# A fused attention and gated-MLP kernel: the output weights loaded earlier, one batch's loads moved back, and more PSUM copies on ScalarE

## The chip, the cores and the metric

The kernel runs on one core of a Trainium2 chip. The metric is the device time of one execution in microseconds (us). TensorE multiplies matrices (PE in the profile, its weight loads PEld), VectorE is DVE, ScalarE is ACT, GpSimd is POOL, and SyncE (SP) only issues DMAs here. Each engine runs its own instructions in program order and waits on semaphores for the others.

## The reference

Eight batches, 12 heads, 448 tokens, head dimension 64. First attention with normalised queries and keys, then a gated MLP in which half of the hidden channels are mixed over the tokens:

```python
q_n, k_n = (rmsnorm(q, g_q), rmsnorm(k, g_k))
scores = scale * np.matmul(q_n, k_n.transpose(0, 1, 3, 2))
attn = softmax(scores)
x = (attn @ v).transpose(0, 2, 1, 3).reshape(B, S, H * D)
h = np.maximum(x @ w_in, 0.0)
u, v = (h[..., :d_ff // 2], h[..., d_ff // 2:])
v_n = (v - mu) / np.sqrt(var + 1e-06)
v_s = np.einsum('ts,bsd->btd', w_spatial, v_n) + b_spatial[None, :, None]
out = (u * v_s) @ w_out
```

(The softmax is written short.) Inputs and output are float32; the matrix products run on bf16.

## The kernel before, in words

**Groups and steps.** The 12 heads of a batch are worked in three groups of four, so there are 24 groups G, three for each batch. A group has seven score pieces of 128 rows. From piece 20 on, pieces are taken in pairs, and one pair is a *step* s, from 10 to 83: a group is 3.5 steps, a batch 10.5. Every step writes its scores into one four-bank PSUM tile, `pss` (L365 and L361), and one exponential on ACT (`expo`, L372) turns it into `et`. As there is only one `pss`, the scores of a step wait for the exponential of the step before. When a group's pieces are through, `attend` (L411) makes the row sums and the weighted values on PE (L394), the reciprocal on ACT (L400, L401) and the product `xt` on DVE (L408). These are the *busy* steps (11, 14, 18, 21 and so on).

**Preparation of q and k.** Each group's q and k go through squares (L237 on POOL, a few on ACT at L235), a reduction on DVE (L245), the inverse root on ACT (L253, L254) and a scaling to bf16, `n`, on POOL (L264). They are then transposed. For the first groups PE does it (L271, copied out on DVE at L278 and L285). From group 6 on SP issues a DMA transpose (L339): q lands straight in `qT`, k lands in `kr`, and DVE scales it into `kT` (L345). A table `todo` says in which step each of these happens, in the order `ks, red, rstd, sc, sq, turn, tr, ld` within a step. For the groups from 9 on, with m = G // 2, an even group's transposes stand in steps 7m-5 and 7m-4, an odd one's in 7m-3 and 7m-2. Groups 6 and 7 have their own: both of group 6 in step 18, both of group 7 in step 20; group 8 has steps 23 and 24, group 9 has 25 and 26.

**Loads of q and k.** Each `load_part` (L107) is one DMA issued from SP. Batch 3 is cut into 22 parts: ten in steps 16 and 17, twelve in steps 21 to 24, three a step. From batch 4 on a batch is ten larger parts, three a step: batch 4 in steps 24 to 27, batch 5 in 34 to 37, batch 6 in 45 to 48. Batches share two buffers in turn, so batch 4 goes where batch 2 was. Within a step, transposes stand before loads, and the stores of finished outputs (`flush`, L529 and L531) come after them, all on SP's one queue.

**The MLP as filler.** Between a step's scores and those of the next, PE is given matmuls of the MLP from a list, `work`, in the steps that aren't busy. `gated(b)` puts a batch's units there: v units (L473), u units (L503), for batch 0 the four PE transposes of the spatial weights (`w_sp_unit`, L205 to L213), for later batches the output units of the batch before (L545), and then the spatial units (L513). Batch 0 is put on the list in step 12, batch 1 in step 22. All units take their PSUM buffers from one pool of four, `ps`, which `attend` and the PE transposes use too. A unit's result is copied out by `relu` (L442 on ACT, L444 on DVE) or `copy` (L448, L450), and `pick` chooses the engine: ACT while a quota lasts, then DVE. Spatial results are multiplied by u on DVE (L517).

**The rest of the first gated part.** In step 12 the spatial weights are loaded by POOL. In step 16 ACT copies the bias row. In step 19 POOL issues the load of `w_out` (L203), one DMA that also casts to bf16. It is first used by the output units of batch 0 that are mixed into `tails(1)` in step 24. The normalised v (`vn`, L495) is made on POOL.

In the profile, the exponentials show the steps: step 10 begins its exponential at 37.71 us, step 16 at 56.75, 17 at 61.40, 18 at 64.30, 19 at 66.90, 20 at 69.79, 21 at 74.82, 24 at 84.83, 30 at 102.45.

Of the kernel before, what the change touches and what calls it, by code (L numbers as in the profile page):

```python
# [19 lines left out]
def kernel(  # L20
# [21 lines left out]
    B, H, S, D = q.shape  # L42
# [8 lines left out]
    pe, act, dve, pool, sync = nc.tensor, nc.scalar, nc.vector, nc.gpsimd, nc.sync  # L51
# [59 lines left out]
    def load_v(b, parts):  # L111
        t = vts[b % 2].rearrange("p h c d -> p h (c d)")
        for i in parts:
            hs = slice(6, 12) if i > 1 else slice(0, 6)
            r, c, n, x = pieces(v[b][hs])[i]
            pool.dma_start(out=t[r, hs, D * c:D * (c + n)], in_=x)  # L116
# [45 lines left out]
    w_spT = const.tile([P, NT, S], BF)  # L162
# [14 lines left out]
    def dummies(n, ps=ps_d):  # L177
        for _ in range(n):
            pe.matmul(out=ps[:, 0:128], lhsT=ident, rhs=ident, start=True, stop=True)
# [17 lines left out]
    def load_w_sp():  # L197
        pool.dma_start(out=w_sp[:, 0:3], in_=moe_w_spatial[0:SM].rearrange("(p c) s -> p c s", c=3))
        pool.dma_start(out=w_sp[0:64, 3], in_=moe_w_spatial[SM:S])
        sync.dma_start(out=bst[64:65, :], in_=moe_b_spatial.partition_broadcast(1))  # L200

    def load_w_out():
        pool.dma_start(out=w_out, in_=moe_w_out.rearrange("(c p) m -> p c m", p=P))  # L203

    def w_sp_unit(sc):  # L205
        ps = ps_w.tile([P, 8, 128], BF, name="ps")
        n = P if sc < 3 else 64
        cols = slice(sc, SM, 3) if sc < 3 else slice(SM, S)
        for t in range(NT):
            kp = P if t < 3 else 64  # L210
            pe.matmul(out=ps[0:n, t, 0:kp], lhsT=w_sp[0:kp, t, cols], rhs=ident[0:kp, 0:kp],
                      is_transpose=True, start=True, stop=True, tile_position=(0, 0))
        dve.tensor_copy(out=w_spT[0:n, sc, :], in_=ps[0:n].rearrange("p t c -> p (t c)")[:, 0:S])  # L213

    def bias_row():
        row, b = w_spT[64:65, NT - 1, :], bst[64:65, :]
        for o, i in ((row[:, 0:SM].rearrange("o (m r) -> o m r", r=P),
                      b[:, 0:SM].rearrange("o (r m) -> o m r", m=3)), (row[:, SM:S], b[:, SM:S])):
            act.activation(out=o, in_=i, func=AF.Copy, bias=0.0, scale=1.0)
# [132 lines left out]
    def scores(ps, p):  # L352
        G, i = divmod(p, NCH)
        y = int(i > 3)
        for yy in ((0, 1) if i == 3 else (y,)):
            qT, kT = qkt[G, 0, yy], qkt[G, 1, yy]
            for h in range(2):
                r = slice(64 * h, 64 * h + 64)
                if i == 3:
                    c0 = 384 + 64 * yy  # L360
                    pe.matmul(out=ps[64 * yy:64 * yy + 64, h, 0:S], lhsT=qkt[G, 1, 0][r, c0:c0 + 64],  # L361
                              rhs=qT[r, :], start=True, stop=True, tile_position=(64 * h, 64 * yy))
                else:
                    c0 = 128 * (i - 4 * y)
                    pe.matmul(out=ps[:, h, 0:S], lhsT=kT[r, c0:c0 + 128], rhs=qT[r, :],  # L365
                              start=True, stop=True, tile_position=(64 * h, 0))

    def expo(ps, p, m):
        s, a = divmod(p, 2)
        if a == 0:  # L370
            ets[s] = e_pool.tile([P, 4, S], BF, name="et")
        act.activation(out=ets[s][:, 2 * a:2 * a + 2 * m, :], in_=ps[:, 0:2 * m, 0:S],  # L372
                       func=AF.Exp, bias=0.0, scale=1.0)
# [37 lines left out]
    def attend(G):  # L411
        for part in (-1, 0, 1):
            weigh(G, part)
            if part < 0:
                recip(G)
        for half in (0, 1):
            xt_store(G, half)
# [14 lines left out]
    quota = [0]  # L432

    def pick():
        if quota[0] > 0:
            quota[0] -= 1
            return act
        return dve
# [7 lines left out]
    def copy(out, in_):  # L446
        if pick() is act:
            act.activation(out=out, in_=in_, func=AF.Copy, bias=0.0, scale=1.0)  # L448
        else:
            dve.tensor_copy(out=out, in_=in_)  # L450
# [82 lines left out]
    def flush():  # L533
        while stores:
            stores.popleft()()
# [37 lines left out]
    def gated(b):  # L573
        work.extend(unit_v(b, 0) + unit_v(b, 1))
        also(lambda: stats(b, 0))
        work.extend(unit_v(b, 2))
        also(lambda: stats(b, 1))
        work.extend(tails(b))
        also(lambda: stats(b, 2))
        also(lambda: stats(b, 3))  # L580
        work.extend(unit_u(b, 0) + unit_u(b, 1))
        also(lambda: ln_rstd(b))
        for c in range(NT):
            also(lambda c=c: ln_apply(b, c))
        work.extend(unit_u(b, 2) + unit_u(b, 3))
        if b == 0:
            work.extend((0.5, lambda sc=sc: w_sp_unit(sc), True) for sc in range(NT))
        else:
            for c in range(3):
                work.extend(unit_o(b - 1, c, 0) + unit_o(b - 1, c, 1))  # L590
        for f in range(4):
            work.extend(unit_s(b, f))
# [3 lines left out]
    def fill(us_of_pe, whole):  # L596

        debt[0] = min(debt[0] + us_of_pe, us_of_pe)
        while work and (debt[0] > 0 or work[0][0] == 0 or (whole and not work[0][2])):
            cost, fn, _ = work.popleft()  # L600
            debt[0] -= cost
            fn()
# [140 lines left out]
    for b in range(2, B):  # L743
        for n, x in enumerate(BY_GROUP if b < 4 else [divmod(n, 5) for n in range(10)]):
            if b == 2:
                step = S0 + n // 4
            elif b == 3:
                step = 16 + n // 5 if n < 10 else 21 + (n - 10) // 3
            else:
                step = (21 * b - 36) // 2 + n // 3  # L750
            todo.setdefault(step, []).append(("ld", NG * b, x))

    ORDER = ("ks", "red", "rstd", "sc", "sq", "turn", "tr", "ld")
# [1 line left out]
    def prep(s, early_act):  # L755
        for what, G, i in sorted(todo.get(s, ()), key=lambda x: (ORDER.index(x[0]), x[1:2] if x[0] == "ld" else x[1:])):
            if (what == "rstd" and G < 5) != early_act:
                continue
            if what == "ld":
                load_part(G // NG, *i)  # L760
            elif what == "turn":
                transpose_pe(G, i, dve)
            elif what == "sq":
                squares(G, i, eng=act if (G, i) in ((6, 1), (7, 1), (8, 1)) else None)
            elif what == "red":
                reduce(G, i)
            elif what == "rstd":
                rstd(G)
            elif what == "sc":
                scaled(G, i, eng=dve if (G, i) in ((4, 0), (4, 1)) else None)  # L770
            elif what == "tr":
                transpose_dma(G, i)
            elif what == "ks":
                k_scale(G)

    def attend_step(G):
        return (NCH * G + NCH - 1) // 2 + 1
# [6 lines left out]
    busy = {attend_step(G) for G in range(NGT)}  # L784
# [6 lines left out]
    for s in range(S0, NST):  # L791
        scores(pss[:, 0:2], 2 * s)
        scores(pss[:, 2:4], 2 * s + 1)
        prep(s, True)
        expo(pss, 2 * s, 2)
        prep(s, False)
        flush()
        if s == S0:
            dummies(24, ps_w.tile([P, 512], FP, name="ps"))
        if s in v_step:  # L800
            load_v(*v_step[s])
        if s == 12:
            load_w_sp()
        if s == 16:
            bias_row()
        if s == 19:
            load_w_out()
        if s in gate_step:
            b = gate_step[s]
            gated(b)  # L810
            nxt = min(x for x in list(gate_step) + [NST] if x > s)
            n = sum(1 for x in range(s, nxt - 1) if x not in busy)
            rate = sum(w[0] for w in work) / (n + 0.5)
        if s in busy:
            attend([G for G in range(NGT) if attend_step(G) == s][0])
            quota[0] = 0
        else:
            quota[0] = 0 if s + 1 in busy else 1
            fill(rate, s + 1 in busy)


# [7 lines left out]
    n = 0  # L829
# [35 lines left out]
```

## Time and profile before

| | |
|---|---|
| median of 5 runs | 295.58 us (293.1 to 299.78) |
| the profiled execution | 298.54 us, span 296.6 us, mean granted TensorE clock 0.988 |
| PE busy | 271.4 us, 92% of the span |
| DVE busy | 212.0 us, 71% |
| ACT busy | 206.1 us, 69% |
| POOL busy | 199.3 us, 67% |
| the 74 exponentials of the steps (L372) | 123.0 us, 1663 ns each |
| SP's queue and ACT's | 40.32 MB in 74562 packets |
| POOL's queue | 8.66 MB in 21744 packets |

The busy shares are averages. To see what one stage is limited by, look at the waits of the engine that is nearly always busy, and follow what released each of them. In the timeline a line is one or more like instructions: start, time, engine, source line, operation, output and inputs, and in brackets how long the engine had been idle and what ended it. SPq lines are DMAs being issued; the time given there is that of the issue, not of the transfer. The DMA rows of the page give the time from issue to landing:

```profile
qb<-in_q_dram SPq DMA_DIRECT2D x38, 96.0 KB, 5.2
kb<-in_k_dram SPq DMA_DIRECT2D x34, 96.0 KB, 5.9
...
w_out<-in_moe_w_out_dram POOLq DMA_DIRECT2D x1, 768.0 KB, 10.0
...
kr<-n SPq DMA_TRANSPOSE x18, 5.4
```

### The profile page before, as it was taken

Reading aid. Unit: us, or ns where it says so; the run is one execution under the profiler, and the core shown is the slowest. Engines: PE = TensorE matmul, PEld = TensorE weight load, DVE = VectorE, ACT = ScalarE, POOL = GpSimd, SP = SyncE. Lnnn points to the kernel's source line nnn. Section 1 sums busy time; section 2 is a strip of 40 time slices with the busy share of each in tenths; the row PEclk is TensorE's granted clock in tenths of the full one; section 3 lists DMA queues with packets and bytes.
Section 4 is the critical chain, followed back from the end, with each engine's and each line's share of the span. In section 5 each row is a group of like instructions: output and inputs, shape, how many; then the busy total and the mean of one; then the engine's idle time right before and its main releaser. Section 6 shows DMA issues by size and latency. Waiting matters only on the chain.

```text
span 296.6 us, 6614 instructions
## 1 busy us (share of the span) xinstructions
PE 271.4 (92%) x2593; PEld 129.8 (44%) x2601; DVE 212.0 (71%) x369; ACT 206.1 (69%) x262; POOL 199.3 (67%) x192
## 2 busy tenths in 40 slices
PE   8588999688979979999999699999999999999994
PEld 8354554333434434444444333444344444444552
DVE  3978777778479486978897648868897949544553
ACT  2798985886857847876877656967787786673411
POOL 3786768999549959589889849489889850400400
PEclk9999999997999999999999989999999999999999
DMA  7998999986999999998889999999971892030145
GB/s 165 226 225 198 193 216 239 221 149 101 147 219 193 250 226 229 245 194 120 198 145 220 222 183 221 231 153 167 165 96 42 133 226 48 24 137 0 30 159 187
DMA packets 97698, 49.99 MB, mean 169 GB/s; under 512 B 67586, under 2 KB 93955, under 8 KB 97667
## 3 DMA queue, kind: packets, MB, share of 16 engines
q1 hardware_dynamic: 74562, 40.32, 65.9%
q0 software_dynamic: 21744, 8.66, 25.2%
q10 hardware_dynamic: 1360, 0.59, 0.8%
q8 instruction: 20, 0.33, 0.5%
q14 instruction: 12, 0.09, 0.1%
HBM read 38.55 MB, written 11.01 MB: 167 GB/s over the span
## 4 chain that ended last, share of the span: by engine, by line
PE 58%; DMA 17%; DVE 7%; ACT 5%; SPq 5%; issue 3%; POOL 3%; ACTq 0%; POOLq 0%; DVEq 0%
PE ps L394 11%; PE ps L473 11%; PE ps L545 10%; PE ps L503 8%; PE ps L513 7%; PE pss L365 7%; DMA qb<-in_q_dram 6%; DMA kb<-in_k_dram 6%; DMA kr<-n 5%; SPq L107 4%; ACT et L372 3%; DVE ms L245 2%; DVE kT L345 1%; DVE xt L408 1%; PE pss L361 1%
## 5 line engine op out<-in xcount | busy, mean ns | idle before, releaser
L372 ACT ACTIVATE et<-pss 128x1792 bf16<-128x1792 f32 x74 | 123.0, 1663 | 55.0 <-PE pss L365 52.3
L545 PE MATMUL ps<-w_out,gt 128*128 128x384 bf16 (+1 forms) x256 | 47.9, 332 | 5.2 <-DVE osb L450 4.8
L264 POOL TENSOR_TENSOR n<-qb,rs 128x896 bf16<-128x896 f32 x19 | 32.0, 1686 | 29.3 <-ACT rs L254 25.4
L245 DVE TENSOR_REDUCE ms<-sqt 128x14 f32<-128x896 f32 x44 | 47.0, 1076 | 5.3 <-POOL sqt L237 4.8
L408 DVE TENSOR_TENSOR xt<-ps,rc 128x448 bf16<-128x448 f32 x48 | 27.8, 618 | 30.3 <-ACT rc L401 30.2
L473 PE MATMUL ps<-w_in_v,xt 128*128 128x512 bf16 (+1 forms) x184 | 45.1, 381 | 0.4
L503 PE MATMUL ps<-xt,w_in_u 128*128 128x448 bf16 x192 | 40.1, 353 | 3.9 <-DMA w_in_u<-in_moe_w_in_dram 2.1
L394 PE MATMUL ps<-et,vt 128*32 128x448 bf16 x768 | 41.0, 353 | 0.5 <-DVE osb L450 0.5
L365 PE MATMUL pss<-qT,kT 64*128 64x448 bf16 x254 | 37.6, 358 | 2.7 <-DVE kT L345 1.7
L237 POOL TENSOR_TENSOR sqt<-qb 128x896 f32<-128x896 f32 x22 | 37.1, 1685 | 0.2
L545 PEld LDWEIGHTS <-gt 128*128 128x128 bf16 (+1 forms) x256 | 24.2, 101 | 25.9 <-issue 13.3
L450 DVE COPY osb<-ps 128x384 f32<-128x384 f32 (+1 forms) x46 | 25.1, 555 | 11.5 <-PE ps L545 10.5
L264 POOL TENSOR_TENSOR n<-kb,rs 128x896 bf16<-128x896 f32 x19 | 32.2, 1693 | 0.1
L237 POOL TENSOR_TENSOR sqt<-kb 128x896 f32<-128x896 f32 x19 | 31.9, 1680 | 0.0
L513 PE MATMUL ps<-w_spT,vn 128*128 128x448 bf16 (+1 forms) x128 | 29.1, 371 | 1.1 <-DVE w_spT L213 1.0
L116 POOL DMA_DIRECT2D vt<-in_v_dram x40 | 29.1, 731 | 1.2 <-PE pss L365 0.7
L495 POOL TENSOR_SCALAR vn<-vs,nm,rv 128x512 bf16<-128x512 bf16 (+1 forms) x32 | 24.1, 767 | 6.6 <-issue 4.4
L503 PEld LDWEIGHTS <-w_in_u 128*128 128x128 bf16 x192 | 17.3, 98 | 24.2 <-issue 10.3
L394 PEld LDWEIGHTS <-vt 128*32 128x32 bf16 x768 | 20.8, 97 | 16.1 <-issue 1.5
L345 DVE TENSOR_SCALAR_CACHE_REDUCE kT<-kr,g_col 128x896 bf16<-128x896 bf16 x18 | 20.5, 1137 | 7.5 <-DMA kr<-n 7.5
L473 PEld LDWEIGHTS <-xt 128*128 128x128 bf16 (+1 forms) x192 | 17.8, 101 | 18.3 <-issue 3.6
L365 PEld LDWEIGHTS <-kT 64*128 64x128 bf16 x276 | 9.9, 94 | 32.3 <-issue 23.6
(88 smaller groups left out, 324.3 us busy)
## 6 DMA issues: line engine op xcount, KB each, us to landing
out_dram<-osb SPq DMA_DIRECT2D x24, 384.0 KB, 4.4
qb<-in_q_dram SPq DMA_DIRECT2D x38, 96.0 KB, 5.2
kb<-in_k_dram SPq DMA_DIRECT2D x34, 96.0 KB, 5.9
qb<-in_q_dram SPq DMA_DIRECT2D x12, 192.0 KB, 4.9
vt<-in_v_dram POOLq DMA_DIRECT2D x8, 288.0 KB, 7.2
vt<-in_v_dram POOLq DMA_DIRECT2D x16, 144.0 KB, 4.9
qb<-in_q_dram SPq DMA_DIRECT2D x4, 576.0 KB, 5.8
qb<-in_q_dram SPq DMA_DIRECT2D x8, 288.0 KB, 6.6
```

The costliest lines, as they stand in the source:

```text
L116: pool.dma_start(out=t[r, hs, D * c:D * (c + n)], in_=x)
L237: pool.tensor_tensor(out=t, in0=x, in1=x, op=ALU.mult)
L245: dve.tensor_reduce(out=sqs[gk][:, key[1], :], in_=sqt.pop(key).rearrange("p h c d -> p (h c) d"), axis=AX.X, op=ALU.add)
L264: (eng or pool).tensor_tensor(out=t.rearrange("p c h d -> p h c d"), in0=raw[key], in1=rst[gk][:, key[1], :].rearrange("p (h c) -> p h c", ...
L365: pe.matmul(out=ps[:, h, 0:S], lhsT=kT[r, c0:c0 + 128], rhs=qT[r, :], start=True, stop=True, tile_position=(64 * h, 0))
L372: act.activation(out=ets[s][:, 2 * a:2 * a + 2 * m, :], in_=ps[:, 0:2 * m, 0:S], func=AF.Exp, bias=0.0, scale=1.0)
L394: pe.matmul(out=ps[32 * l:32 * l + 32, 0:S], lhsT=w, rhs=et_of(G, 3 if r == 3 else r + 4 * y, h), start=(r == 0), stop=(r == 3), tile_posi ...
L408: dve.tensor_tensor(out=xts[b][:, 2 * g + half, :], in0=pst.pop((G, half))[:, 0:S], in1=rec[G], op=ALU.mult)
L473: pe.matmul(out=ps[0:m, :], lhsT=xts[b][:, j, t0:t0 + m], rhs=w_in_v[:, j, :], start=(j == 0), stop=(j == 5), tile_position=(0, 0))
L503: pe.matmul(out=ps[:, 0:S], lhsT=w_in_u[:, j, 128 * f:128 * f + 128], rhs=xts[b][:, j, :], start=(j == 0), stop=(j == 5))
L513: pe.matmul(out=ps[:, 0:S], lhsT=vn_t[b % 2][0:kp, c, 128 * f:128 * f + 128], rhs=w_spT[0:kp, c, :], start=(c == 0), stop=(c == NT - 1))
L545: pe.matmul(out=ps[o:o + m, 0:384], lhsT=gts[b][f][:, t0:t0 + m], rhs=w_out[:, f, r], start=(f == 0), stop=(f == 3), tile_position=(0, o))
```

## The change

Three edits. The copy of the transposed spatial weights now goes through `copy`, so that `pick` chooses its engine, and before step 18 the quota is 2 in each step that isn't busy. Before, it was 1, or 0 in the step ahead of a busy one; from step 18 on that stays. The loads of batch 4 go from steps 24 to 27 to steps 26 to 29. The load of `w_out` goes from step 19 to step 16, after the bias row.

```diff
@@ -210,7 +210,7 @@
-        dve.tensor_copy(out=w_spT[0:n, sc, :], in_=ps[0:n].rearrange("p t c -> p (t c)")[:, 0:S])
+        copy(w_spT[0:n, sc, :], ps[0:n].rearrange("p t c -> p (t c)")[:, 0:S])
@@ -747,7 +747,7 @@
             elif b == 3:
                 step = 16 + n // 5 if n < 10 else 21 + (n - 10) // 3
             else:
-                step = (21 * b - 36) // 2 + n // 3
+                step = {4: 26}.get(b, (21 * b - 36) // 2) + n // 3
@@ -803,7 +803,6 @@
         if s == 16:
             bias_row()
-        if s == 19:
             load_w_out()
@@ -815,7 +814,8 @@
         else:
-            quota[0] = 0 if s + 1 in busy else 1
+
+            quota[0] = 2 if s < 18 else 0 if s + 1 in busy else 1
             fill(rate, s + 1 in busy)
```

## The prediction

> **What bounds the kernel now.** I read the busy table first (PE 92%), then the chain of waits, then TensorE's own waits by stage. The chain from 128 us to the end is mostly PE lines; before that it runs through loads, SP's queue and `kr` transposes. TensorE runs its program in order, so only what makes PE stand still counts. The larger idle stretches of PE from 53 us on: 2.09 at 55.3 (`w_in_u` landing), 1.03 at 60.2, 1.05 at 70.2, 1.66 at 84.4, 0.47 at 88.8, 2.51 at 105.9, 2.27 at 169.5. From the timelines of PE and of VectorE (start, duration, instruction; the bracket is idle time before it and what ended it):
>
> ```profile
> 70.21 4.08 PE L513 MATMUL ps<-w_spT,vn 128*128 128x448 bf16 x11 [1.05 <-DVE w_spT L213]
> ...
> 82.40 0.36 PE L365 MATMUL pss<-qT,kT 64*128 64x448 bf16 x2
> 84.42 0.36 PE L365 MATMUL pss<-qT,kT 64*128 64x448 bf16 x2 [1.66 <-DVE kT L345]
> ...
> 105.85 1.30 PE L545 MATMUL ps<-w_out,gt 128*128 128x384 bf16 x7 [2.51 <-DVE osb L450]
> ```
>
> ```profile
> 83.21 1.15 DVE L345 TENSOR_SCALAR_CACHE_REDUCE kT<-kr,g_col 128x896 bf16<-128x896 bf16 x1 [2.97 <-DMA kr<-n]
> ...
> 103.18 1.15 DVE L345 TENSOR_SCALAR_CACHE_REDUCE kT<-kr,g_col 128x896 bf16<-128x896 bf16 x1 [2.31 <-DMA kr<-n]
> 104.25 0.08 DVE L345 DVE_READ_ACCUMULATOR kT<-kr,g_col 128x1 f32 x1
> 104.25 1.08 DVE L245 TENSOR_REDUCE ms<-sqt 128x14 f32<-128x896 f32 x1
> 105.25 0.55 DVE L450 COPY osb<-ps 128x384 f32<-128x384 f32 x1
> ```
>
> The reader is to see that both large stalls are one thing. VectorE stands waiting for a transpose `kr` to land. At 84.4 PE needs that very `kT` (group 7). At 105.9 it needs a PSUM buffer whose copy to `osb` is queued on VectorE behind group 9's `kT`. Why were the two transposes late? POOL's and SP's timelines:
>
> ```profile
> 69.09 1.69 POOL L264 TENSOR_TENSOR n<-qb,rs 128x896 bf16<-128x896 f32 x1 [0.36 <-ACT rs L254]
> 70.73 0.85 POOL L203 DMA_DIRECT2D w_out<-in_moe_w_out_dram  x1
> 71.61 1.70 POOL L264 TENSOR_TENSOR n<-kb,rs 128x896 bf16<-128x896 f32 x1
> ```
>
> ```profile
> 90.54 2.14 SPq L339 DMA_TRANSPOSE qT<-n  x1
> 92.72 1.27 SPq L107 DMA_DIRECT2D qb<-in_q_dram  x2
> 94.09 2.19 SPq L107 DMA_DIRECT2D kb<-in_k_dram  x1
> 96.38 0.79 SPq L531 DMA_DIRECT2D out_dram<-osb  x1
> 97.26 1.85 SPq L339 DMA_TRANSPOSE kr<-n  x1
> ```
>
> Group 7: the `w_out` issue stands between the two scalings on POOL, and its packets (786 KB, 72.6 to 80.4 us) share the DMA engines with qT(7) (issued 70.81, landed 79.01: 8.20 us) and kr(7) (issued 73.33, used at 83.21: up to 9.9). The pair just before, without `w_out`, took 3.07 and 3.03. Group 9: its normalised K was ready at 90.42 on POOL, but SP issued the transpose at 97.26, after qT(9), three batch-4 loads and a store; three more batch-4 loads were issued just before qT(9), at 88.5 to 90.4.
>
> **What the Trainium skill says.** "DMA: Bandwidth & Descriptors", section "Issuing engines are not separate DMA queues": DMAs from SP, ACT and POOL run on the same 16 engines and interleave. The trace agrees: 3.07 against 8.20 us. Same page, "Queues, rings and completion order": on each engine a queue's descriptors are consumed in ring order. The trace agrees: SP's landings from 84 to 103 us follow the order of issue. "TensorE: Matmul & The Clock Gate", Part 1: an idle window of about 3.4 us halves the clock, and the window is free-running. Here the granted clock was 0.5 for 3.41 us from 70.85 and from 169.84, each after a stall, so about 1.7 us of PE time each; the 2.51 stall brought none. So a stall may cost more than its length, and not in every run.
>
> **The change, part by part.** All durations are of the profiled execution: 298.54 us, span 296.6, 1.94 around it. That is 2.96 above the median of the five runs (295.58), so I sum on 298.54 and scale.
>
> *More PSUM copies on ACT.* Before, the quota was 0 in steps 13 and 17, 1 in 12, 15, 16 and 19. With 2, counting which units end in which step (from PE's timeline): v1 and v2 (step 13), u1 (16), u2 and u3 (17) move from DVE to ACT. Because the transposed-weight copy now calls the same chooser, its second one (step 19) moves too. w_sp0 comes third in step 17 and stays on DVE, as do v3 (third in step 13) and w_sp2, w_sp3. Steps 10 and 15 have no copies to move. DVE loses 2 x 0.60 + 3 x 0.55 + 0.38 = 3.2 us of work, but PE's waits there come from `w_in_u` (DMA) and from qT(5), which itself waited for POOL squares: I give the relief nothing (bounds: 0 to -1.0, the gap at 60.2). ACT gains about 5 x 0.57 (row L442) plus one copy of 128x448 bf16. The nearest rows are the same copy on DVE (0.38) and 128x896 on ACT (0.92); I take 0.5. Steps 13 and 16 hide theirs in ACT's idle 2.46 and 0.96 us. Steps 17 to 20 do not; ACT runs there without a gap:
>
> ```profile
> 62.96 0.31 ACT L253 ACTIVATE ln<-ms,eps 128x28 f32<-128x28 f32 x1
> 63.30 0.23 ACT L254 ACTIVATE rs<-ln 128x28 f32<-128x28 f32 x1
> 63.45 0.95 ACT L235 ACTIVATE sqt<-kb 128x896 f32<-128x896 f32 x1
> 64.30 1.65 ACT L372 ACTIVATE et<-pss 128x1792 bf16<-128x1792 f32 x1
> ```
>
> u2 and u3 go between 63.45's square and the exponential of step 18, which then starts at 65.44. The single score buffer is free at 67.1, so PE's scores of step 19, at 66.17 now, stand 0.95. Reciprocal, exponential, rstd(7) and square follow, each 1.14 later; the w_sp1 copy then ends near 71.5, where DVE's ended at 70.16. So PE's first big spatial run starts at 71.5 instead of 70.21: **+1.3** (0 if ACT's copies hide after all; +1.8 with POOL's delay below on DVE's reduction).
>
> *w_out at step 16.* Its 0.85 us moves to POOL at 60.41, ahead of the four vn scalings (60.78) and everything up to group 7. vn is used from 68.2, so that is covered; qT(6) goes from 65.48 to 66.3, kr(6) from 67.36 to 67.95. The transfer would start about 62.3 (issue plus 1.85, as now), beside batch-3 loads that are in flight until 66.4; DMA moved only 82 GB/s from 63 to 67 us, so there is room. 786 KB at some 127 GB/s while loads share (42 to 48 us shows that for POOL's queue), then up to 167: nearly done at 68.5. kr(6) then lands near 72.8 (bounds: 70.9 with no delay, 77.8 if it takes kr(7)'s 9.9), its kT is ready at 74.0, and scores of group 6 begin at 74.22 + 1.3 = 75.5. No stall. kr(7), issued about 73.8 because ACT's rstd(7) is later, has no `w_out` beside it and lands near 77.5, before DVE reaches it at 80.2. PE arrives at the place of the first stall at 82.76 + 1.3 = 84.06 instead of being released at 84.42: **-0.4**; if the slow-clock stretch at 70.85, now hidden in that stall, doesn't recur, 1.7 more: -2.1. I take the middle, **-1.2** net of the +1.3. With kT(7) on time DVE's backlog is gone, and the 0.47 wait at 88.8: **-0.4**.
>
> *Batch 4 two steps later.* Ten SP issues (0.6 to 0.7 us each; 3, 3, 3, 1) move from steps 24-27 to 26-29. Steps 24 and 25 hold kr(8) and qT(9); kr(9) is first in step 26. So six loads, and their data, leave the way: kr(9) can be issued near 90.5 and lands by about 95 even at 4.1 us like kr(8) plus a little, far before DVE reaches it at 100.87. DVE then does kT(9) to 102.0, the reduction to 103.05 and the osb copy to 103.55; PE wants it at 103.34. **-2.3** (bounds -2.5, and 0 if another transfer holds kr(9) beyond 103). The loads were all issued by 102.0; now SP reaches them at about 92 and ends before that. Group 12's squares (step 33) have four steps, as batch 5 has now. No transposes are due in steps 27 to 29. Stores of batch 0 are flushed from step 30, behind the last load; nothing waits for them soon. Batch 6, at 45-48, keeps the same collision: the 2.27 at 169.5 stays.
>
> Sum: -1.2 - 0.4 - 2.3 = **-3.9**, from -3.1 to -4.8 with the clock. After 107 us PE is dense, and what it needs is paced by it, so the lead should last. 298.54 - 3.9 = 294.6; times 295.58/298.54: **291.7 us**.
>
> **Rivals.** (1) *The stall moves to group 6.* `w_out` overlaps kr(6) more than I think; it lands at 76, kT at 77.2, and PE, which needs 8.5 us from there, is at the old place at 85.7: +1.3, with -2.3 from batch 4: 297.5, scaled 294.6. For it: qT(7)'s 8.20. Against: the light DMA at 63-67. (2) *Slower.* The same place, price higher: kr(6) takes all of kr(7)'s 9.9, lands at 77.8, kT at 79.0, PE reaches the old place at 87.4, +3.0, and gt evacuations stuck behind kT on DVE add about 0.5: +1.2 after batch 4's gain, 299.7, scaled 296.7. It turns to a loss when kr(6) lands later than about 77.2. (3) *The gain is given back*: the lead of PE at 107 meets a later landing, most likely kr(15) at 166.8, since DMA carries 200 GB/s there; -0.5 to -1.5 remains, about 294.8. This includes that the later loads buy kr(9) nothing because batch 3's loads alone hold it.
>
> **How the numbers follow.** Forecast 0.55 (own range 289.5 to 293.3), rival 1 0.20, rival 2 0.15, rival 3 0.10. About 1% is what a measurement of this kernel can tell from no change; that bound is 292.6. Faster: 0.46 of the forecast and 0.03 of rival 1. Slower: the upper part of rival 2 and unforeseen ACT or POOL delays, 0.15. Same: 0.36. The range runs from 288.8 (no slow clock at all, all three gains) to 296.8 (rival 2).
>
> **What would show it.** Right: no PE wait for kT at group 7 and none for osb in step 30; kr(9) issued within 2 us of its scaling; `w_out` landed by 72; a hole of about a microsecond before the scores of step 19 and a longer one before the spatial matmuls. Wrong: a wait for kT or qT of group 6 before the scores of step 21; kr(9) still landing after 100; DVE still idle on `kr` there.

## The result, and the profile after

The changed kernel takes 297.26 us (median of 28 runs, 294.21 to 301.28), the kernel before 296.77 us in the runs beside it. The ratio is **1.0044**, 95% interval 1.002 to 1.0069: 0.4% slower. Both kernels have slower executions as well; the ratio compares only those within 1.5% of each kernel's fastest (20 of the 28 here), so it is not the ratio of the two medians, and the profiled execution before, 298.54 us, is one of those left out. The forecast was 291.7 us, so an expected gain of 3.9 us became a loss of 1.3.

Yet both stalls that the forecast meant to remove are gone. This is the PE timeline of the changed kernel, at the places of the two stalls and a little later:

```profile
85.68 0.55 PE L365 MATMUL pss<-qT,kT 64*128 64x448 bf16 x4
...
102.85 2.56 PE L545 MATMUL ps<-w_out,gt 128*128 128x384 bf16 x13
...
114.28 2.98 PE L473 MATMUL ps<-w_in_v,xt 128*128 128x512 bf16 x13
119.96 0.93 PE L365 MATMUL pss<-qT,kT 64*128 64x448 bf16 x4 [2.70 <-DVE kT L345]
120.82 1.31 PE L394 MATMUL ps<-et,ones 128*32 128x448 bf16 x12
```

The scores of step 24 now run as four matmuls in one line, without the wait for group 7's `kT`, and the 13 output matmuls of step 30 without the wait for `osb`. At step 31 the exponential starts at 105.94 us, against 107.67 before: PE is 1.7 us ahead, after having been 1.1 behind at step 17. Then a new wait stands before the scores of step 35: 2.70 us for `kT` of **group 10**. Step 36's exponential starts at 124.99 us against 122.53, so five steps have turned a lead of 1.7 into a lag of 2.5. The last line above shows the rest of the price: 12 matmuls in 1.31 us, where they took 0.75 before. The granted clock is 0.50 from 119.6 to 123.0 us. Later the two profiles differ once more: the one before has its wait of 2.27 us at 169.5 us (step 51), and this one hasn't. So this execution ends 0.9 us earlier (spans 295.7 and 296.6 us) although the kernel is the slower one. Nothing in the change touches step 51; that wait comes and goes between executions, as the point on the sum shows further down.

VectorE and SP of the changed kernel say why group 10 is late:

```profile
112.82 0.62 DVE L517 TENSOR_TENSOR gt<-ps,us 128x448 bf16<-128x448 f32 x1
118.75 1.15 DVE L345 TENSOR_SCALAR_CACHE_REDUCE kT<-kr,g_col 128x896 bf16<-128x896 bf16 x1 [5.30 <-DMA kr<-n]
```

```profile
94.17 1.28 SPq L339 DMA_TRANSPOSE kr<-n  x1
95.50 3.48 SPq L107 DMA_DIRECT2D qb<-in_q_dram  x5
99.08 5.56 SPq L107 DMA_DIRECT2D kb<-in_k_dram  x5
104.75 3.26 SPq L339 DMA_TRANSPOSE qT<-n  x1
108.12 0.51 SPq L529 DMA_DIRECT2D out_dram<-osb  x1
108.72 3.98 SPq L339 DMA_TRANSPOSE kr<-n  x1
```

SP with group 10's pair before:

```profile
103.96 1.26 SPq L339 DMA_TRANSPOSE qT<-n  x1
105.86 0.39 SPq L529 DMA_DIRECT2D out_dram<-osb  x1
106.34 1.85 SPq L339 DMA_TRANSPOSE kr<-n  x1
```

Group 9's `kr` now goes ahead of batch 4's loads and lands at 97.63. But the ten loads, in one block from 95.5 to 104.6, now stand in front of group 10's pair. These transposes take 3.26 and 3.98 us merely to issue (1.26 and 1.85 before), and land 10.9 and 10.0 us after the start of their issue (5.58 and 7.19 before). So `kr` is issued 2.4 us later and lands 5.2 us later. DVE stands 5.30 us.

The same is seen in the DMA columns. The view gives, for a stretch, its length, each engine's busy time and count, then the granted clock, the DMA load and GB/s. The load is the time that all packets took as a share of the 16 DMA engines' time; packets that overlap are each counted, so it can exceed 1. Before, and then changed:

```profile
80.00:86.00 6.00, 4.34 (x28) 1.73 (x25) 3.03 (x6) 3.33 (x3) 3.33 (x2) 1.00 1.21 173
108.00:118.00 10.00, 9.95 (x92) 4.25 (x92) 6.82 (x12) 7.77 (x8) 8.04 (x7) 1.00 1.32 237
```

```profile
80.00:86.00 6.00, 5.95 (x44) 2.13 (x33) 5.60 (x9) 4.47 (x6) 2.69 (x2) 1.00 0.14 37
108.00:118.00 10.00, 9.21 (x86) 3.61 (x84) 2.71 (x5) 6.13 (x6) 9.62 (x7) 1.00 1.57 183
```

With `w_out` gone to 62 to 71 us, the DMA engines have almost nothing to do from 80 to 86 us (37 GB/s). At 108 to 118, where batch 4's tail, batch 3's v and three output stores meet group 10's transposes, their load is higher than before (1.57 against 1.32) and they move less (183 GB/s against 237).

### The profile page after: what moved, and what is told of

Same layout as the page of the kernel before. It is cut to its first block, busy times and chain, and to the rows that moved or that the text cites. A ratio compares the mean times of both kernels' runs of the same rounds, so it can differ in the third digit from the quotient of the medians.

```text
span 295.7 us, 6613 instructions
## 1 busy us (share of the span) xinstructions
PE 274.0 (93%) x2593; PEld 130.6 (44%) x2601; DVE 209.2 (71%) x363; ACT 209.1 (71%) x268; POOL 199.4 (67%) x192
## 4 chain that ended last, share of the span: by engine, by line
PE 57%; DMA 20%; DVE 7%; ACT 6%; SPq 3%; POOL 2%; issue 2%; POOLq 0%; ACTq 0%; DVEq 0%
DMA qb<-in_q_dram 12%; PE ps L394 11%; PE ps L503 11%; PE ps L545 10%; PE ps L473 9%; PE ps L513 8%; PE pss L365 7%; DMA kb<-in_k_dram 5%; SPq L107 3%; DMA kr<-n 3%; ACT et L372 3%; DVE ms L245 2%; DVE xt L408 2%; PE pss L361 1%; DVE kT L345 1%
## 5 line engine op out<-in xcount | busy, mean ns | idle before, releaser
L372 ACT ACTIVATE et<-pss 128x1792 bf16<-128x1792 f32 x74 | 123.0, 1663 | 50.5 <-PE pss L365 46.3
L545 PE MATMUL ps<-w_out,gt 128*128 128x384 bf16 (+1 forms) x256 | 47.1, 327 | 0.7 <-DVE gt L517 0.3
L503 PEld LDWEIGHTS <-w_in_u 128*128 128x128 bf16 x192 | 17.3, 98 | 24.4 <-issue 10.5
```

The costliest lines, as they stand in the source:

```text
L503: pe.matmul(out=ps[:, 0:S], lhsT=w_in_u[:, j, 128 * f:128 * f + 128], rhs=xts[b][:, j, :], start=(j == 0), stop=(j == 5))
L545: pe.matmul(out=ps[o:o + m, 0:384], lhsT=gts[b][f][:, t0:t0 + m], rhs=w_out[:, f, r], start=(f == 0), stop=(f == 3), tile_position=(0, o))
```

## The experiments

Theory A: each edit acts alone, where the forecast put it. Theory B: PE's lead is given back at the next transpose that is late; for the moved loads, because they now stand in front of it. Theory C: holes in PE's work cost more than their length, through the halved clock. All ratios are against the kernel before, with 95% intervals.

**Each edit alone, and the two load moves together.** The first run (e1_quota) takes the quota and the weight copy:

```diff
-        dve.tensor_copy(out=w_spT[0:n, sc, :], in_=ps[0:n].rearrange("p t c -> p (t c)")[:, 0:S])
+        copy(w_spT[0:n, sc, :], ps[0:n].rearrange("p t c -> p (t c)")[:, 0:S])
...
-            quota[0] = 0 if s + 1 in busy else 1
+            quota[0] = 2 if s < 18 else 0 if s + 1 in busy else 1
```

> Only the quota and the weight copy through the chooser; the loads stay. Theory A (each edit acts alone where I placed it): PE waits about 0.6 to 1.0 us before the scores of step 19 and starts the spatial run of step 20 about 1.3 us later; some of this hides in group 7's kT stall, so +0.3 to +1.3 us, ratio 1.001 to 1.004. Theory B (these copies cost nothing because PE waits there for POOL and DMA anyway): ratio 0.999 to 1.001.

Measured: **1.0051** (1.0015 to 1.0088). The trace has both holes where the forecast placed them (PE, then ACT, of this kernel):

```profile
67.97 0.38 PE L361 MATMUL pss<-qT,kT 64*64 64x448 bf16 x4 [0.62 <-ACT et L372]
...
72.32 3.93 PE L513 MATMUL ps<-w_spT,vn 128*128 128x448 bf16 x11 [1.21 <-ACT w_spT L448]
```

```profile
65.41 0.96 ACT L442 ACTIVATE us<-ps 128x448 bf16<-128x448 f32 x2
66.25 1.67 ACT L372 ACTIVATE et<-pss 128x1792 bf16<-128x1792 f32 x1
...
71.75 0.53 ACT L448 ACTIVATE w_spT<-ps 128x448 bf16<-128x448 bf16 x1
```

Two more copies stand ahead of an exponential that had no gap before it, and PE waits for that exponential. The second copy of `w_spT` runs on ACT, behind a square, instead of on DVE. Theory A holds for this part, at a cost slightly above its range.

The load of `w_out` alone (e2_wout):

```diff
-        if s == 19:
+        if s == 16:
             load_w_out()
```

> Only the load of w_out, step 16 instead of 19. Theory A: group 7's transposes land in 3 to 5 us instead of 8 to 10, no PE wait for kT of group 7, -1.5 to -2.5 us, ratio 0.992 to 0.995. Theory B (what PE gains there is given back at the next transpose that is late): the wait for kT of group 7 goes, one of the later waits grows by as much, ratio 0.998 to 1.002.

Measured: **1.0051** (1.0023 to 1.0079). No wait for group 7 is left, but PE waits 1.38 us for `kT` of group 6, which now shares the engines with `w_out`, and the wait for `osb` in step 30 grows from 2.51 to 4.13: PE comes earlier and group 9's `kr`, still behind batch 4's loads, doesn't. Theory B, and a higher cost than it said.

The loads of batch 4 alone (e3_b4):

```diff
-                step = (21 * b - 36) // 2 + n // 3
+                step = {4: 26}.get(b, (21 * b - 36) // 2) + n // 3
```

> Only the loads of batch 4, two steps later. Theory A: no PE wait for osb in step 30, and none for kT of group 10, -2.3 us, ratio 0.992. Theory B (the wait moves): the wait for osb in step 30 goes, the loads are then in front of group 10's transposes, which take 8 us or more, and PE waits 2 to 4 us for kT of group 10 before the scores of step 35: ratio 0.998 to 1.006.

Measured: **0.9996** (0.9965 to 1.0028). The wait in step 30 is gone. Group 10's `kr` took 8.26 us and landed at 114.12, in time by about a microsecond in this execution. So the wait that theory B expected isn't there, only a lesser one of 0.88 for a PSUM buffer at 120 us. But this execution (293.55 us) is the fastest of the kernel's 22, whose median is 295.88, and over all of them the time falls by nothing that can be measured. Whether the slower ones have the wait this trace can't say, so where the 2.5 us went stays open. The ratio is in theory B's range, its wait isn't seen.

The two edits of the loads together, the quota as before (e4_wout_b4):

> w_out and batch 4 moved, the quota as before. Theory A: -3.5 to -4.5 us, ratio 0.985 to 0.988. Theory B: PE ahead by some 2 to 4 us at step 31 and a wait for kT of group 10 that takes most of it, ratio 0.995 to 1.001; the whole change minus this one is then the cost of the quota, 0.3 to 0.6%.

Measured: **1.0121** (1.0052 to 1.0189, six runs). This is beyond what either theory named. PE waits 3.16 us for `kT` of group 10, whose transposes took 10.5 and 9.8 us, and the clock is halved for 6.83 us twice, from 71.9 (after a 1.87 us hole before the spatial units) and from 119.7 (after that wait). The two moves that alone cost 0.5% and nothing cost 1.2% together. The timed runs show the clock too: the mean granted clock of those compared is 0.974, against 0.986 before. And the quota that the whole change adds to this kernel doesn't make it dearer: the whole change is at 1.0044, although the two intervals just overlap. A possible reading: the more PE leads, the fuller the DMA engines are when group 10's pair is due. The next runs test the second half of it, the traffic.

**Room for the moved loads.** If that is the cause, it should help to take other traffic from there and put it in the empty 80 to 86 us. Batch 3's v, five POOL loads in steps 28 to 32, goes to a buffer that is free after step 21's attention. Added to the kernel with both load moves (e5_v3):

```diff
-        if b + 2 < B:
+        if b + 2 < B and b != 1:
...
+        if s == 22:
+            load_v(3, range(5))
         prep(s, False)
```

> w_out at 16, batch 4 at 26, the quota as before, and the five loads of batch 3's v all at the head of step 22 instead of in steps 28 to 32. Theory B (the gain is given back because the moved batch-4 loads, v and the stores come at once at 95 to 120 us, right where group 10's transposes are due, while DMA is idle at 80 to 86 us): group 10's transposes land in 5 to 8 us instead of 10, the wait for its kT of 2.7 to 3.2 us shrinks to below 1, and with it the half-clock stretch near 120: 3 to 5 us less than the same kernel with v in place (1.012 of before), ratio 0.996 to 1.002. Theory C (the time goes to the half clock that the hole before the spatial units, step 20, sets off at 72 us, whatever comes after): the wait shrinks, but the ratio stays above 1.005.

Measured: **0.9895** (0.9867 to 0.9923). The same two edits cost 1.2% without this one and gain 1.05% with it; the intervals are far apart. No wait for group 10 is left, and no half-clock stretch after 14 us but the one in the tail. Theory B was right in sign and better than its numbers. Theory C alone is refuted: the two kernels are the same program up to step 22, and the hole before the spatial units is 1.87 us here as well.

The control, v at step 22 in the kernel before and nothing else (e12_v3_only):

> The kernel before with only batch 3's v at step 22. Group 9's kr still stands behind the six batch-4 loads on SP, so theory B expects the wait for osb in step 30 to stay at 2 us or more, and v to slow group 7's kr further: ratio 0.998 to 1.004. If v's place alone is what e5_v3 gained by: ratio 0.988 to 0.993.

Measured: **1.0194** (1.0121 to 1.0266, six runs), dearer than either expectation. v's place is no gain in itself. In this kernel the stretch from 80 to 86 us isn't empty (173 GB/s in the profile before). v shares 80 to 91 us with batch 3's loads and with group 8's transposes, which land 6.3 and 5.2 us after their issue (5.4 and 4.1 before); group 9's `kr` still waits behind batch 4's loads, and the wait for `osb` in step 30 is 4.23 us. The clock is halved for 6.83 us from 107.8, still within that wait. How much of the 5.7 us each of these makes up isn't shown.

The whole change, with v moved too (e10_all_v3):

> The whole change as it was made, with only batch 3's v moved to the head of step 22. Theory B: the 2.7 us wait for kT of group 10 goes and so does the half-clock stretch at 120 us; 1.0 to 1.5% below the whole change (1.0044), ratio 0.990 to 0.995; what is left against e5_v3 (0.9895) is the quota, 0.2 to 0.5%. If the quota's holes were what undid the change, it stays at 1.001 to 1.005.

Measured: **0.9905** (0.9875 to 0.9936), median 292.74 us, as expected; with e5_v3 it is the fastest version (e11_b4_v3 and e9_b6 below beat both kernels too, by less). SP, DVE and the DMA stretches of this kernel, in the fastest of its 15 executions:

```profile
103.16 2.84 SPq L339 DMA_TRANSPOSE qT<-n  x1
106.11 0.51 SPq L529 DMA_DIRECT2D out_dram<-osb  x1
106.72 2.88 SPq L339 DMA_TRANSPOSE kr<-n  x1
```

```profile
112.46 1.15 DVE L345 TENSOR_SCALAR_CACHE_REDUCE kT<-kr,g_col 128x896 bf16<-128x896 bf16 x1 [1.63 <-DMA kr<-n]
```

```profile
80.00:86.00 6.00, 6.00 (x41) 2.41 (x39) 5.58 (x12) 4.83 (x8) 4.95 (x6) 1.00 1.45 170
108.00:118.00 10.00, 9.95 (x105) 4.00 (x98) 7.21 (x14) 7.03 (x8) 7.51 (x5) 1.00 1.16 272
```

The hole is filled (170 GB/s), the later stretch is loaded less and moves more (272), `kr` lands 5.72 us after its issue, and DVE's 1.63 us wait is over before PE needs the result. From step 34's exponential to step 39's this kernel takes 16.31 us (e5_v3 16.50) and the changed kernel 19.98: the 3.67 between them is most of the 4.1 us between the two ratios.

The other traces agree. Where batch 4's loads are moved and v isn't (four kernels), group 10's `kr` lands 8.3 to 10.0 us after its issue; where v is moved too (five), 5.5 to 6.4; where the loads stay (six), 5.2 to 7.2. It takes the loads and v together: here the block of loads still stands right in front of the pair, and PE doesn't wait. Nor is it POOL's time for issuing v that is gained, since `kr` is issued no sooner: 6.2 us after step 30's exponential here, 5.6 in the changed kernel. No run lets the transposes go ahead of the moved loads, so what the place in the queue adds to the traffic isn't known.

One thing differs from the expectation: against e5_v3's 0.9895 the quota seems to cost nothing here, though 0.2% could hide in the intervals. The hole before the spatial units is 1.87 us there and 1.21 here. A possible reading is that with `w_out` ahead on POOL, VectorE's copies are late anyway; but e2_wout, the same program as e5_v3 up to there, has a hole of only 0.2 us, so this isn't shown. What the ratios show is that the quota's cost and `w_out`'s don't add.

Batch 4 and v moved, `w_out` back in step 19 (e11_b4_v3):

> Batch 4 at 26 and batch 3's v at step 22, w_out still in step 19. w_out is then in flight at 72 to 80 us and v at 80 to 86, beside group 7's transposes and batch 3's loads. If w_out's move is worth its place once v makes room: 0.3 to 0.8% slower than e5_v3, ratio 0.993 to 0.998, with the wait for kT of group 7 of 1.4 us or more. If w_out's move is worth nothing (alone it was 1.005): ratio 0.987 to 0.991.

Measured: **0.9943** (0.9903 to 0.9982), with the wait for group 7's `kT` of 1.60 us. As expected if `w_out`'s move is worth its place once there is room, but the interval overlaps that of e5_v3: 0.5% is likely, not shown.

**The holes at step 20 and the clock.** The kernel before, with group 8's first reduction a step later, so that VectorE's weight copies go ahead of it (e6_red):

```diff
-             8: {"sq": (18, 19), "red": (19, 20)}}
+             8: {"sq": (18, 19), "red": (20, 20)}}
```

> The kernel before, with one reduction (group 8's q) moved from step 19 to 20, so that VectorE's copies of the spatial weights no longer stand behind it. Theory C (PE's hole of 1.05 us before the spatial units costs its length and, in most runs, a half-clock stretch of 3.4 us, 1.7 us of PE time): no hole over 0.3 us at step 20, mean granted clock up by 0.003 to 0.006, ratio 0.991 to 0.997. If group 7's kT wait takes the gain back (theory B): hole gone, wait for kT longer by as much, ratio 0.998 to 1.002.

Measured: **1.0021** (0.9989 to 1.0054). The hole is gone and step 21 starts at 73.7 instead of 74.8 us; step 24 starts at the same 84.8, since PE waits 0.92 us for a PSUM buffer that `gt` frees, and then for group 7's `kT` all the same. Theory B.

The same line added to e5_v3 (e7_v3_red):

> w_out at 16, batch 4 at 26, v of batch 3 at step 22, group 8's first reduction at step 20, quota as before. If theories B and C are both right, neither the hole at step 20 nor the waits for group 7, for osb in step 30 and for group 10 are over 0.5 us, clock 0.990 or better, ratio 0.980 to 0.990. If waits only move: ratio above 0.995.

Measured: **0.9979** (0.9952 to 1.0006), worse than without it. PE of this kernel:

```profile
72.47 2.27 PE L513 MATMUL ps<-w_spT,vn 128*128 128x448 bf16 x11
77.72 0.55 PE L365 MATMUL pss<-qT,kT 64*128 64x448 bf16 x4 [2.98 <-DVE kT L345]
```

The spatial run starts with no hole, and 2.98 us of waiting for group 6's `kT` stand right after it; from 78.8 us the clock is halved for 6.83. When one cause of a hole is taken away, the next one holds PE at nearly the same place. The clock wasn't halved there in e5_v3's trace, after its hole of 1.87 us.

The quota of 2 before step 17 alone, weight copies on VectorE (e8_quota16):

> Only the quota of 2, and only before step 17, with the weight copies on VectorE: v1, v2 and u1 move to ScalarE, u2, u3 and the second weight copy stay. If the quota's 0.5% comes from step 17 to 20, where ScalarE has no gap, as I worked it out: ratio 0.998 to 1.002 and no wait for et before the scores of step 19. If it comes from the earlier copies: ratio 1.003 or more.

Measured: **0.9976** (0.9941 to 1.0012), no wait for `et` before the scores of step 19. So v1, v2 and u1 move to ACT at no cost that can be measured. That the quota's 0.5% lies in what runs from step 17 on is likely: the trace says so, and the intervals of the two runs are apart, but barely (e1_quota's begins at 1.0015).

The wait for group 10's `kT` itself, filled. Here `dummies` issues 32 matmuls that nothing reads, in the whole change (e13_fill):

```diff
+        if s == 35:
+            dummies(32, ps_w.tile([P, 512], FP, name="ps"))
         scores(pss[:, 0:2], 2 * s)
```

> The whole change with 32 matmuls of 128x128 (about 2 us) that nothing reads put before the scores of step 35, where PE waits 2.7 us for kT of group 10. They leave the transposes, the loads and the queues as they are. If the clock that is halved after such a wait is a real part of what the wait costs: the stretch near 120 us is gone, the mean clock rises by 0.003 to 0.006, 0.5 to 1.7 us less than the whole change, ratio 0.998 to 1.003. If the wait costs only its own length: ratio 1.004 to 1.008, as the change or a little above it.

Measured: **1.0026** (0.999 to 1.0062). The wait left is 0.59 us, the stretch at 120 us is gone in the trace, and the mean clock of the timed runs compared is 0.990, against 0.984 in the changed kernel. The ratio lies where the expectation put it if the clock counts. But its interval takes in the change's 1.0044, and the trace has new waits of 1.04 and 0.29 us for PSUM buffers behind the filler: the clock's share of the loss isn't shown by the times.

**One step further.** e5_v3's two moves made for batch 6 as well (loads at 47, batch 5's v at step 43; e9_b6). The wait for `osb` that the expectation puts in step 47 stands in step 51 by the exponentials; it is the one at 169.5 us before.

> As e5_v3, and the same pair of moves for batch 6: its loads two steps later (47 instead of 45) and batch 5's v at the head of step 43 instead of in 49 to 53. Theory B (every such pair has its loads in front of an odd group's kr, and the moved loads then need room that v gives up): the wait for osb in step 47 (2.0 us in e5_v3) goes and nothing takes its place, 1 to 2 us below e5_v3, ratio 0.983 to 0.988. If the lead is given back at a later kr: 0.988 to 0.992, with a new wait after 170 us.

Measured: **0.9948** (0.9913 to 0.9983). The trace has no wait in step 51 and its span is 291.0 us against e5_v3's 293.0; the medians are the same (293.62 and 293.49). The expected gain didn't come, and why is open.

## Why the prediction was wrong, point by point

- **What bounds the kernel now.** Right: the two largest waits of the middle stage were late transposes, and late for the two reasons given. Both went in every trace in which their causes went.
- **More copies on ACT, +1.3.** Right in mechanism and place when the part stands alone. Forecast were 0.95 at step 19 and the spatial run 1.3 later; the changed kernel shows 0.63, and a run that starts 9.83 us after step 17's exponential, against 8.81 before: 1.0 later. The part alone costs 0.5%, 1.5 us, and e8_quota16 agrees that the copies called free are free. Wrong is the sum: beside the earlier `w_out` this cost isn't added.
- **w_out at step 16.** The path came nearly as worked out: issued at 61.51, landed at 70.9 (forecast: nearly done at 68.5), group 6's `kr` landed at 73.29 (72.8), and group 7's wait went. Yet the move, a gain in the sum, costs 0.5% on its own (1.0051). The sum credited PE with arriving early and took no account of what it arrives early *for*: rival 1's wait for group 6 (1.38 us in e2_wout), then group 9's `kr`.
- **Batch 4 two steps later, -2.3.** This is the step that failed. The forecast said that SP would reach the loads at 92 and be done before 102, that no transposes are due in steps 27 to 29, and that group 12 has time. It checked the stage that the loads leave and the consumer of the loads, not the stage that they enter. SP reached the loads at 95.5 and had issued the last at 104.64, and the next users of the queue, qT(10) and kr(10) in steps 30 and 31, took 10.9 and 10.0 us where the profile before had 5.58 and 7.19. Loads that had been spread over 88.5 to 102 in gaps between transposes had become one block, and v and the stores came on top. The transposes of group 10 appear nowhere in the sum. On its own the move measured 0 (0.9996), not -2.3.
- **"The lead should last."** Wrong for the same reason: PE lost its lead at the wait for kr(10). This is rival 3's mechanism (chance 0.10), but not its place or size: it named kr(15), some 48 us later, and left a gain of 0.5 to 1.5 us. That the mechanism is the right one is shown by e5_v3 and e10_all_v3: moving five loads out of that stage turns 1.0121 into 0.9895 and 1.0044 into 0.9905.
- **The clock.** The forecast named the halved clock as a chance to gain 1.7 us. In the changed kernel's profile it is a cost: from 50 us to the tail, 6.83 us at half speed from 71.8 and 3.41 from 119.6, at the holes that the change made or moved. If PE is limiting throughout, that is 5.1 us, against 3.4 in the profile before. Over the timed runs little of this is left: the mean clock of those compared is 0.984, against 0.986 before. And e10_all_v3, the same program up to step 22 with the same hole of 1.21 us, keeps the full clock there, so the stretch at 71.8 doesn't follow from the change in every execution.
- **The sum.** It was made against one profiled execution, 298.54 us, that was 1.8 us above the later median. The wait in step 30 is 2.51 there and 1.48 to 2.72 in e1_quota, e6_red and e8_quota16, which leave it alone; the wait in step 51 is 2.27 there and between none and 2.15 in the others that leave batch 6 alone. Even the way to step 17 varies: 61.4 us in the profile before, 62.8 to 64.4 in the traces of e3_b4, e6_red, e11_b4_v3 and e12_v3_only, which are the same program up to there. A stall read from one trace is one draw.

## What to carry to other kernels

When transfers are moved away from a place where they do harm, look at what is due in the place where they go: list every transfer of the same stage, the queue they stand in and the next dependent one behind them, as carefully as for the place that is relieved. When DMA is busy most of the time, a lead of the compute engine is not a gain until the transfers that it will need next are early too; look for a hole in the DMA row and fill that, as here at 80 to 86 us (in the kernel before, where that stretch isn't empty, v in the same place cost 1.9%). Costs and gains of edits that act on one wait don't add; try the pair before summing the parts.

## What the runs showed of the hardware that had not been expected

- A 128x896 bf16 transpose took 3.0 us from issue to landing with little else in flight (group 6 before: 3.07 and 3.03), 8 beside the `w_out` load (group 7 before: 8.20), and 10 to 11 behind ten queued loads with v and stores beside them (group 10 in the changed kernel: 10.9 and 10.0); in that state SP needed 3.3 to 4.0 us to issue one, against 1.26 for qT(10) before.
- The half-clock stretches between 50 us and the tail last 3.41 or 6.83 us: one or two of the free-running windows of about 3.4 us that the Trainium skill describes ("TensorE: Matmul & The Clock Gate", Part 1), so in length the trace agrees with it. But where that page speaks of an idle window, no window had to be idle throughout here: all but two of the waits beside these stretches are shorter than 3.4 us, the shortest 1.04 and 1.05. Each stretch began during a wait of 1 us or more or within 1.3 us after it, but not every such wait brought one: 2.51 us brought none in the profile before, 1.05 did. In 39 timed runs of the kernel before, the mean granted clock and the time go together (correlation -0.59, 1.2 us for each 0.01).
